# A dense SiLU block on one core: block 1 of x loaded behind the first w1 group, block 0 multiplied alone

## The chip, the core and the metric

The kernel runs on one core of one Trainium2 chip. The metric is the device time of one execution in microseconds (us). Five runs of the kernel before gave 127.13, 127.39, 127.45, 128.46 and 128.78, so the median is 127.45. Beside them there is one profiled execution, from which all durations below are taken.

## The reference

```python
# x: 1 x 2048 x 640, w1: 640 x 1728, w2: 1728 x 640, all bfloat16
def reference(x, w1, w2):
    h = jnp.einsum("bsd,df->bsf", x, w1)
    h = _silu(h)
    out = jnp.einsum("bsf,fd->bsd", h, w2)
    return out
```

## The kernel before

**Names.** S = 2048 rows of x, D = 640 features (DT = 5 tiles of 128), F = 1728 hidden units (FT = 13 full tiles of 128 and a tail of 64). The rows of x are cut into NSC = 4 chunks of 512. `xT` holds x transposed (features on partitions), `w1s` and `w2s` the weights, `hT` the hidden layer, transposed. PSUM has 8 banks, handed out in turn by `bank()`.

**Work.** TensorE (PE) multiplies in two phases. In the first, each tile of 128 hidden units is accumulated over the 5 feature tiles, with w1 as the stationary operand and `xT` streamed; ScalarE (ACT) applies SiLU on the way from PSUM to `hT`. In the second phase the hidden layer is multiplied with w2; VectorE (DVE) and ACT bring results out of PSUM, and SyncE (SP) issues the stores. Chunks 1 to 3 of x arrive transposed by transposing loads (line 149). Chunk 0 is loaded as it is, in blocks of 128 rows (`x0`), and turned on PE against an identity matrix.

**The lead-in**, which the change is about, is an order written out by hand:
- Line 124 loads block 0 of x on SP's queue; line 125 loads block 1 on ACT's queue. Line 126 puts ACT's share of the start-up barrier behind that load. All loads go through the helper at line 89.
- Lines 127 to 131 load w1 in four groups of hidden tiles on SP's queue, `G = [(0, 2), (2, 5), (5, 9), (9, 13)]` (320, 480, 640 and 720 KB). Line 132 loads blocks 2 and 3 of x behind them. After these come the 15 transposing loads of line 149 and the loads of w2.
- Lines 193 and 197 run `dummies(n)`: n matmuls over a tile of zeros, 256 columns each, whose result nobody reads (line 164).
- `turn(j, b_v, b_a)` (lines 166 to 190) waits for block j, transposes its five 128 x 128 tiles into PSUM (line 173), and copies them to `xT`: three tiles on DVE (line 176), two on ACT (line 184), or all five on DVE where both banks are the same.
- `half(ft, m, c0)` (line 216) multiplies m hidden tiles, from tile ft on, with 256 rows of x from row c0 on, and gives the bank to SiLU. All matmuls are recorded under line 200, all of these SiLUs under line 204.
- Line 230 waits for blocks 0 and 1 to be turned; the loop at line 232 then does all 13 tiles on rows 0 to 255, with a wait for the w1 group before each step and the turns of blocks 2 and 3 behind tiles 9 and 11.

[...]

Of the kernel before, what the change touches and what calls it, by code (L numbers as in the profile page):

```python
# [9 lines left out]
def bass_standalone__dense_activation_silu__prompt_kernel(  # L10
# [13 lines left out]
    P = 128  # L24
    NB = 8
    BANK = 512
    DT = D // P
# [3 lines left out]
    HB = 256  # L31
# [6 lines left out]
    pe, act, dve, pool, sp = nc.tensor, nc.scalar, nc.vector, nc.gpsimd, nc.sync  # L38

    with ExitStack() as es:  # L40
        def sb(name, shape, dtype):
            return es.enter_context(nc.sbuf_tensor(name, shape, dtype))

        xT = sb("xT", [P, DT, S], bf16)
        x0 = sb("x0", [P, SCH // P, D], bf16)
        w1s = sb("w1s", [P, DT, F], bf16)
        w2s = sb("w2s", [P, FT, D], bf16)
        w2t = sb("w2t", [P, D], bf16)
        hT = sb("hT", [P, FT, S], bf16)
# [6 lines left out]
        ps = es.enter_context(nc.psum_tensor("ps", [P, NB, BANK], fp32))  # L56
# [4 lines left out]
        def sem(name):  # L61
            s = es.enter_context(nc.semaphore(name))
            count[s.name if hasattr(s, "name") else name] = 0
            return [s, 0]

        def tick(ins, s, n=1):
            ins.then_inc(s[0], n)
            s[1] += n
            return (s, s[1])

        def wait(eng, *points):
            for pt in points:
                if pt is None:
                    continue
                s, v = pt
                key = (id(eng), id(s))
                if seen.get(key, 0) < v:
                    eng.wait_ge(s[0], v)
                    seen[key] = v

        s_pe, s_act, s_dve = sem("s_pe"), sem("s_act"), sem("s_dve")
# [4 lines left out]
        def load(eng, out_ap, in_ap):  # L86
            s = sem(f"s_ld{n_dma[0]}")
            n_dma[0] += 1
            return tick(eng.dma_start(out=out_ap, in_=in_ap), s, 16)  # L89

        ET = mybir.EngineType

        def preamble(engine, opcode):
            lst = nc.main_func.blocks[0].instructions
            return next(
                i for i, ins in enumerate(lst)
                if ins.opcode == opcode and ins.engine == engine
            )
# [12 lines left out]
        def barrier_wait_here(engine):  # L111
            lst = nc.main_func.blocks[0].instructions
            lst.append(lst.pop(preamble(engine, "EventSemaphore")))

        x_v = xf.rearrange("(j p) d -> p j d", p=P)
# [5 lines left out]
        ld_x = {}  # L121
        ld_w1 = {}
        p_z = ahead_of_start(lambda: tick(dve.memset(z[:, :], 0.0), s_dve), ET.DVE)  # L123
        ld_x[0] = load(sp, x0[:, 0, :], x_v[:, 0, :])
        ld_x[1] = load(act, x0[:, 1, :], x_v[:, 1, :])
        barrier_wait_here(ET.Activation)
        for a, b in G:
            e = F if b == FT else b * P
            pt = load(sp, w1s[:, :, a * P:e], w1_v[:, :, a * P:e])
            for ft in range(a, b):  # L130
                ld_w1[ft] = pt
        ld_x[2] = ld_x[3] = load(sp, x0[:, 2:4, :], x_v[:, 2:4, :])
        barrier_wait_here(ET.SP)

        p_warm = tick(pool.memset(warm[:, :], 0.0), s_pool)
        p = tick(pool.memset(ident[:, :], 0.0), s_pool)
# [9 lines left out]
        for c in range(1, NSC):  # L146
            s = sem(f"s_xc{c}")
# [14 lines left out]
        def dummies(n):  # L162
            for _ in range(n):
                pe.matmul(ps[:, 3, 0:HB], lhsT=z[:, 0:P], rhs=z[:, :], start=True, stop=True)  # L164

        def turn(j, b_v, b_a):
            wait(pe, ld_x[j], p_ident, bank_free[b_v], bank_free[b_a])
            v = ps[:, b_v, :].bitcast(bf16)
            a = ps[:, b_a, :].bitcast(bf16)
            nv = DT if b_a == b_v else 3  # L170
            for dt in range(DT):
                dst = v[:, dt * P:(dt + 1) * P] if dt < nv else a[:, (dt - nv) * P:(dt - nv + 1) * P]
                ins = pe.transpose(dst, x0[:, j, dt * P:(dt + 1) * P], ident[:, :])  # L173
            t = tick(ins, s_pe)
            wait(dve, t)
            r = tick(dve.tensor_copy(  # L176
                out=xT[:, 0:nv, j * P:(j + 1) * P],
                in_=v[:, 0:nv * P].rearrange("p (k s) -> p k s", s=P),
            ), s_dve)
            bank_free[b_v] = r  # L180
            pts = [r]
            if nv < DT:
                wait(act, t)
                r = tick(act.copy(  # L184
                    out=xT[:, nv:DT, j * P:(j + 1) * P],
                    in_=a[:, 0:(DT - nv) * P].rearrange("p (k s) -> p k s", s=P),
                ), s_act)
                bank_free[b_a] = r
                pts.append(r)
            return pts  # L190

        wait(pe, p_z)
        dummies(7)
        barrier_wait_here(ET.PE)
        t0 = turn(0, 7, 6)
        t1 = turn(1, 5, 4)
        dummies(2)

        def mm(o, l, r, start, stop, shared=False):
            return pe.matmul(o, lhsT=l, rhs=r, start=start, stop=stop, skip_group_check=shared)  # L200

        def silu(out_ap, in_ap, bank, after):
            wait(act, after)
            r = tick(act.activation(out=out_ap, in_=in_ap, func=ACT.Silu), s_act)  # L204
            bank_free[bank] = r
            return r
# [3 lines left out]
        def bank():  # L210
            b = nxt[0] % NB
            nxt[0] += 1
            wait(pe, bank_free[b])
            return b

        def half(ft, m, c0):
            b = bank()
            for i in range(m):
                for k in range(DT):
                    ins = mm(  # L220
                        ps[:, b, i * HB:(i + 1) * HB],
                        w1s[:, k, (ft + i) * P:(ft + i + 1) * P],
                        xT[:, k, c0:c0 + HB],
                        start=(k == 0 and i == 0), stop=(k == DT - 1), shared=True,
                    )
            t = tick(ins, s_pe)
            silu(hT[:, ft:ft + m, c0:c0 + HB],
                 ps[:, b, 0:m * HB].rearrange("p (m s) -> p m s", m=m), b, t)

        wait(pe, *t0, *t1)  # L230
        tb = []
        for ft, m in [(0, 2), (2, 1), (3, 2), (5, 2), (7, 2), (9, 1), (10, 1), (11, 1), (12, 1)]:
            wait(pe, ld_w1[ft])
            half(ft, m, 0)
            if ft in (9, 11):
                b = bank()
                tb.extend(turn(2 if ft == 9 else 3, b, b))
# [3 lines left out]
        for c in range(1, NSC):  # L241
            wait(pe, ld_xc[c])
            for ft in range(FT):
                b = bank()
                for k in range(DT):
                    ins = mm(ps[:, b, :], w1s[:, k, ft * P:(ft + 1) * P],
                             xT[:, k, c * SCH:(c + 1) * SCH], start=(k == 0), stop=(k == DT - 1))
                h_last = silu(hT[:, ft, c * SCH:(c + 1) * SCH], ps[:, b, :], b, tick(ins, s_pe))
        h_tail = []
        for q in range(NSC // 2):  # L250
            b = bank()
            for k in range(DT):
                for hh in range(2):
                    c = 2 * q + hh
                    ins = mm(ps[hh * FL:(hh + 1) * FL, b, :], w1s[:, k, F0:F],
                             xT[:, k, c * SCH:(c + 1) * SCH],
                             start=(k == 0), stop=(k == DT - 1), shared=True)
# [18 lines left out]
        for c in range(NSC):  # L276
            b = bank()
            wbank.append(b)
            for ft in range(FT):
                mm(ps[:, b, :], w2s[:, ft, DA:D], hT[:, ft, c * SCH:(c + 1) * SCH],  # L280
                   start=(ft == 0), stop=False)
# [59 lines left out]
        for q in range(NSC // 2):  # L341
            tt = []
            for hh in range(2):
                c = 2 * q + hh
# [3 lines left out]
            for hh in range(2):  # L348
                c = 2 * q + hh
# [42 lines left out]
```

## Time and profile before

| What | Value |
|---|---|
| Profiled execution, its own time | 127.13 us |
| Span from its first to its last instruction | 125.7 us |
| Median of five runs (lowest, highest) | 127.45 us (127.13, 128.78) |
| PE matmuls L200, w1 phase (345) | 59.8 us busy |
| PE matmuls L200, w2 phase, `hT` streamed (221) | 45.4 us busy |
| PE dummies L164 (9) | 2.3 us busy, mean 418 ns |
| PE transposes L173 (20) | 2.1 us busy, mean 264 ns |
| HBM read, written | 5.16 MB, 2.62 MB |

Times are counted from the first instruction of the span. PE is tensor matmuls, PEld the loads of their stationary operand, which overlap the matmuls. Matmuls are pipelined: the duration of one is longer than the distance to the next, so the pace is read from the number of instructions in a stretch of time. A DMA row says from which queue a transfer was issued (SPq, ACTq); q1 and q10 are the rings that serve SP's and ACT's queues. A row of the timeline gives start, length, engine, line, operation, tiles and count, and in brackets the idle time before it and what ended it.

### The profile page before, as it was taken

How to read it: one execution, taken by the hardware profiler on the slowest of the kernel's cores; microseconds unless marked ns; L12 is line 12 of the kernel's file. 1: busy time of each engine (PE TensorE's matmuls, PEld its weight loads, DVE VectorE, ACT ScalarE, POOL GpSimd, SP SyncE). 2: the span in 40 equal slices, each digit the busy share in tenths (PEclk: the TensorE clock that was granted, in tenths of full speed). 3: DMA queues.
4: the chain of work that ended last, by engine and by line, in shares of the span. 5: the costliest groups of instructions: out<-in, count | busy, mean ns of one | idle time of the engine just before them, and what ended most of it. 6: DMA issues, size and time to landing. Idle time of an engine off the chain costs nothing.

```text
span 125.7 us, 1522 instructions
## 1 busy us (share of the span) xinstructions
PE 122.5 (97%) x668; PEld 62.3 (50%) x668; DVE 9.2 (7%) x16; ACT 40.3 (32%) x71; POOL 0.8 (1%) x7
## 2 busy tenths in 40 slices
PE   8899999999999999999999999999999999999993
PEld 5589886444444444444444443444344444444452
DVE  0101100000000000000000004202020210012021
ACT  5256456555555555555540003010101011010100
POOL 2000000000000000000000000000000000000000
DMA  6999535479600000000000000542111111111112
GB/s 188 344 383 202 92 87 115 91 160 389 228 1 0 0 0 3 0 5 0 0 0 0 0 0 16 114 124 75 52 52 52 52 52 52 57 52 52 52 55 102
DMA packets 17830, 10.37 MB, mean 83 GB/s; under 512 B 10784, under 2 KB 17824, under 8 KB 17824
## 3 DMA queue, kind: packets, MB, share of 16 engines
q1 hardware_dynamic: 17536, 10.05, 27.5%
q10 hardware_dynamic: 288, 0.23, 0.6%
q8 instruction: 5, 0.08, 0.3%
q14 instruction: 1, 0.01, 0.0%
HBM read 5.16 MB, written 2.62 MB: 62 GB/s over the span
## 4 chain that ended last, share of the span: by engine, by line
PE 95%; DMA 3%; SPq 0%; issue 0%; ACT 0%
PE ps L200 94%; DMA w1s<-in_w_dram 3%; PE ps L173 0%; SPq L89 0%; ACT o_sb L269 0%; SPq L377 0%
## 5 line engine op out<-in xcount | busy, mean ns | idle before, releaser
L200 PE MATMUL ps<-xT,w1s 128*128 128x512 bf16 (+2 forms) x345 | 59.8, 342 | 0.6 <-DMA w1s<-in_w_dram 0.5
L200 PEld LDWEIGHTS ps<-xT,w1s 128*128 128x128 bf16 (+1 forms) x345 | 32.9, 99 | 27.1 <-DVE xT L176 1.3
L200 PE MATMUL ps<-w2s,hT 128*128 128x512 bf16 (+2 forms) x221 | 45.4, 367 | 0.0
L204 ACT ACTIVATE hT<-ps 128x512 bf16<-128x512 f32 (+1 forms) x55 | 31.4, 574 | 27.6 <-PE ps L200 27.6
L200 PEld LDWEIGHTS ps<-w2s,hT 128*128 128x128 bf16 x221 | 20.9, 98 | 24.4 <-issue 1.1
L269 ACT CAST o_sb<-ps 128x512 bf16<-128x512 f32 (+1 forms) x8 | 4.4, 546 | 42.2 <-PE ps L200 42.2
L200 PE MATMUL ps<-hT,w2s 128*128 128x512 bf16 x52 | 11.4, 379 | 0.0
L267 DVE CAST o_sb<-ps 128x512 bf16<-128x512 f32 (+1 forms) x9 | 6.1, 677 | 39.9 <-PE ps L200 39.9
L200 PEld LDWEIGHTS ps<-hT,w2s 128*128 128x128 bf16 x52 | 5.0, 97 | 6.3 <-issue 0.4
L267 DVE CAST oT<-ps 128x512 bf16<-128x512 f32 x2 | 1.3, 686 | 63.4 <-PE ps L200 63.4
L269 ACT CAST oT<-ps 128x512 bf16<-128x512 f32 x2 | 1.1, 588 | 11.1 <-PE ps L200 11.1
L164 PE MATMUL ps<-z 128*128 128x256 bf16 x9 | 2.3, 418 | 0.4 <-DVE z L123 0.4
L176 DVE COPY xT<-ps 128x384 bf16<-128x384 bf16 (+1 forms) x4 | 1.7, 425 | 10.9 <-PE ps L173 10.9
L173 PE MATMUL ps<-ident,x 128*128 128x128 bf16 x20 | 2.1, 264 | 0.2 <-DMA x<-in_x_dram 0.2
L200 PE MATMUL ps<-w2t,hTt 64*128 64x512 bf16 (+2 forms) x17 | 2.2, 366 | 0.0
L173 PEld LDWEIGHTS ps<-ident,x 128*128 128x128 bf16 x20 | 1.6, 116 | 0.8 <-DMA x<-in_x_dram 0.7
L204 ACT ACTIVATE hTt<-ps 128x512 bf16<-128x512 f32 x2 | 1.2, 597 | 1.1 <-PE ps L200 1.1
L143 ACT ACT_TABLE_LOAD x1 | 1.3, 1283 | 0.7 <-PEq L377 0.7
L164 PEld LDWEIGHTS ps<-z 128*128 128x128 bf16 x9 | 1.1, 142 | 0.7 <-DVE z L123 0.4
L200 PEld LDWEIGHTS ps<-w2t,hTt 64*128 64x128 bf16 x17 | 0.7, 94 | 1.4 <-issue 0.8
L184 ACT COPY xT<-ps 128x256 bf16<-128x256 bf16 x2 | 0.7, 372 | 1.0 <-PE ps L173 1.0
L200 PE MATMUL ps<-hTt,w2t 64*128 64x512 bf16 x4 | 0.6, 382 | 0.0
(10 smaller groups left out, 1.5 us busy)
## 6 DMA issues: line engine op xcount, KB each, us to landing
out_dram<-o_sb SPq DMA_DIRECT2D x15, 160.0 KB, 1.8
w2s<-in_w_dram SPq DMA_DIRECT2D x1, 1120.0 KB, 6.0
w2s<-in_w_dram SPq DMA_DIRECT2D x1, 960.0 KB, 8.9
w1s<-in_w_dram SPq DMA_DIRECT2D x1, 720.0 KB, 7.2
w1s<-in_w_dram SPq DMA_DIRECT2D x1, 640.0 KB, 5.9
w1s<-in_w_dram SPq DMA_DIRECT2D x1, 480.0 KB, 4.8
w1s<-in_w_dram SPq DMA_DIRECT2D x1, 320.0 KB, 3.9
x<-in_x_dram SPq DMA_DIRECT2D x1, 320.0 KB, 7.0
```

The costliest lines, as they stand in the source:

```text
L143: act.activation(out=warm[:, :], in_=warm[:, :], func=ACT.Silu)
L164: pe.matmul(ps[:, 3, 0:HB], lhsT=z[:, 0:P], rhs=z[:, :], start=True, stop=True)
L173: ins = pe.transpose(dst, x0[:, j, dt * P:(dt + 1) * P], ident[:, :])
L176: r = tick(dve.tensor_copy(out=xT[:, 0:nv, j * P:(j + 1) * P], in_=v[:, 0:nv * P].rearrange("p (k s) -> p k s", s=P),), s_dve)
L184: r = tick(act.copy(out=xT[:, nv:DT, j * P:(j + 1) * P], in_=a[:, 0:(DT - nv) * P].rearrange("p (k s) -> p k s", s=P),), s_act)
L200: return pe.matmul(o, lhsT=l, rhs=r, start=start, stop=stop, skip_group_check=shared)
L204: r = tick(act.activation(out=out_ap, in_=in_ap, func=ACT.Silu), s_act)
L267: r = tick(dve.tensor_copy(out=out_ap, in_=in_ap), s_dve)
L269: r = tick(act.copy(out=out_ap, in_=in_ap), s_act)
```

## The change

Block 1 of x is loaded on SP's queue, between the first and the second w1 group, no longer on ACT's queue; the line that moved ACT's barrier goes with it. The dummies at the start become 9, and 3 follow the turn of block 0 where 2 followed the turn of block 1. The first two hidden tiles are no longer multiplied with 256 rows at once: `first_block(ft, j)` multiplies hidden tile ft with the 128 rows of block j, and four calls fill the same bank. Between them block 1 is turned. The order on PE is now: 9 dummies, turn of block 0, 3 dummies, tile 0 on block 0, turn of block 1, tile 1 on block 0, a wait for block 1's copies, tile 0 and tile 1 on block 1, then the loop as before from tile 2 on. In the changed file the matmuls carry line 199 and the SiLUs of `half` line 203.

```diff
--- before.py
+++ after.py
@@ -122,13 +122,13 @@
         ld_w1 = {}
         p_z = ahead_of_start(lambda: tick(dve.memset(z[:, :], 0.0), s_dve), ET.DVE)
         ld_x[0] = load(sp, x0[:, 0, :], x_v[:, 0, :])
-        ld_x[1] = load(act, x0[:, 1, :], x_v[:, 1, :])
-        barrier_wait_here(ET.Activation)
         for a, b in G:
             e = F if b == FT else b * P
             pt = load(sp, w1s[:, :, a * P:e], w1_v[:, :, a * P:e])
             for ft in range(a, b):
                 ld_w1[ft] = pt
+            if a == 0:
+                ld_x[1] = load(sp, x0[:, 1, :], x_v[:, 1, :])
         ld_x[2] = ld_x[3] = load(sp, x0[:, 2:4, :], x_v[:, 2:4, :])
         barrier_wait_here(ET.SP)
 
@@ -190,11 +190,10 @@
             return pts
 
         wait(pe, p_z)
-        dummies(7)
+        dummies(9)
         barrier_wait_here(ET.PE)
         t0 = turn(0, 7, 6)
-        t1 = turn(1, 5, 4)
-        dummies(2)
+        dummies(3)
 
         def mm(o, l, r, start, stop, shared=False):
             return pe.matmul(o, lhsT=l, rhs=r, start=start, stop=stop, skip_group_check=shared)
@@ -227,9 +226,25 @@
             silu(hT[:, ft:ft + m, c0:c0 + HB],
                  ps[:, b, 0:m * HB].rearrange("p (m s) -> p m s", m=m), b, t)
 
-        wait(pe, *t0, *t1)
+        def first_block(ft, j):
+            for k in range(DT):
+                c = ft * HB + j * P
+                ins = mm(ps[:, 0, c:c + P], w1s[:, k, ft * P:(ft + 1) * P],
+                         xT[:, k, j * P:(j + 1) * P],
+                         start=(k == 0 and ft == 0 and j == 0), stop=(k == DT - 1), shared=True)
+            return ins
+
+        bank()
+        wait(pe, *t0, ld_w1[0])
+        first_block(0, 0)
+        t1 = turn(1, 5, 4)
+        first_block(1, 0)
+        wait(pe, *t1)
+        first_block(0, 1)
+        t = tick(first_block(1, 1), s_pe)
+        silu(hT[:, 0:2, 0:HB], ps[:, 0, :].rearrange("p (m s) -> p m s", m=2), 0, t)
         tb = []
-        for ft, m in [(0, 2), (2, 1), (3, 2), (5, 2), (7, 2), (9, 1), (10, 1), (11, 1), (12, 1)]:
+        for ft, m in [(2, 1), (3, 2), (5, 2), (7, 2), (9, 1), (10, 1), (11, 1), (12, 1)]:
             wait(pe, ld_w1[ft])
             half(ft, m, 0)
             if ft in (9, 11):
```

## The prediction

> **What bounds the kernel now.** I read the page's engine totals first, then the chain of waits in order of time, then the timeline of the first 16 us, then the transfers there. The totals name the engine:
>
> ```profile
> PE 122.5 (97%) x668; PEld 62.3 (50%) x668; DVE 9.2 (7%) x16; ACT 40.3 (32%) x71; POOL 0.8 (1%) x7
> ```
>
> TensorE (PE) is busy for 122.5 of 125.7 us, so only the lead-in can hold a loss. The chain (start us, length us, what) shows it:
>
> ```profile
> 0.09 0.39 SPq L89
> 0.47 0.06 issue
> 0.53 3.85 DMA w1s<-in_w_dram
> 4.38 0.14 issue
> 4.52 6.24 PE ps L200 x50
> 10.76 0.28 PE ps L173 x5
> 11.04 1.09 PE ps L200 x10
> 12.13 0.28 PE ps L173 x5
> ```
>
> The first w1 group is issued at 0.53, lands at 4.38, and the first real matmul starts at 4.52. Ten matmuls over 256 columns then take 1.09, so one goes every 0.109 us; five 128-column transposes take 0.28, or 0.056 each. Fifty at 0.109, of which the last lasts 0.27, would be 5.61; the row says 6.24. The missing 0.63 lies at the start, as two windows show (length, then PE busy, then weight loads):
>
> ```profile
> 4.51:5.74 1.23, 1.22 (x6) 0.87 (x7) 0.00 (x0) 0.00 (x0) 0.00 (x0) 1.00 1.08 366
> 6.23:7.76 1.53, 1.53 (x17) 1.36 (x14) 0.00 (x0) 0.93 (x2) 0.00 (x0) 1.00 1.08 387
> ```
>
> Fourteen loads fit in 1.53 (0.109 each), but only six matmuls in 1.23, about 0.21 each. Some 6 matmuls cost 0.104 too much: 0.63. The clock column says 1.00 in both windows, so the two paces are read from the instructions alone. The pace doubles near 5.8. Before that:
>
> ```profile
> 0.39 1.68 PE L164 MATMUL ps<-z 128*128 128x256 bf16 x7 [0.39 <-DVE z L123]
> 2.29 1.26 PE L173 MATMUL ps<-ident,x 128*128 128x128 bf16 x10 [0.22 <-DMA x<-in_x_dram]
> 3.04 0.36 DVE L176 COPY xT<-ps 128x384 bf16<-128x384 bf16 x1 [2.70 <-PE ps L173]
> 3.04 0.37 ACT L184 COPY xT<-ps 128x256 bf16<-128x256 bf16 x1 [0.79 <-PE ps L173]
> 3.34 0.63 PE L164 MATMUL ps<-z 128*128 128x256 bf16 x2
> 4.52 6.24 PE L200 MATMUL ps<-xT,w1s 128*128 128x256 bf16 x50 [0.54 <-DMA w1s<-in_w_dram]
> ```
>
> Seven dummies in 1.68, the last lasting 0.42, go every 0.21; ten transposes about every 0.107, half the pace they have at 10.76. PE stands still for 0.22 before block 0 and 0.54 before w1. The transfers set that last gap and the deadlines behind it (KB, us from issue to landing):
>
> ```profile
> w1s<-in_w_dram SPq DMA_DIRECT2D x1, 640.0 KB, 5.9
> w1s<-in_w_dram SPq DMA_DIRECT2D x1, 480.0 KB, 4.8
> x<-in_x_dram SPq DMA_DIRECT2D x1, 320.0 KB, 7.0
> ```
>
> With issues at 0.99, 1.56 and 3.19, w1 group 2 lands at 5.8, group 3 at 7.5 and x blocks 2 and 3 at 10.2. In the window 1.1 to 2.5 the ACT queue (q10, x block 1) shares the 16 DMA engines with SP's (q1):
>
> ```profile
> q1 hardware_dynamic: 295, 0.24, 61.3%
> q10 hardware_dynamic: 144, 0.16, 33.6%
> ```
>
> **The change, part by part.** All of it is made against this execution: 127.13 us with a span of 125.7, the fastest of five, 0.32 under their median. My yardstick is when the group of row tile 2 can start: 10.76 less one duration (0.27) less 39 x 0.109 = 6.24.
>
> *Block 1 leaves the ACT queue and goes behind w1 group 1.* q10's packets took 33.6% of 1.4 us = 0.47 us of all engines, mostly ahead of w1's. So group 1 lands up to 0.47 sooner, and not sooner at all if issue-to-first-packet time holds it. I take 0.40, nearer the busy end because the two shares together, 94.9% over the window, leave little idle: landing 3.98, first matmul 0.14 later (as now) at 4.12. Block 1 then lands when all the bytes before it have: still 4.38, usable at 4.52; bounds 4.3 and 4.85 (a full 0.47 behind an unmoved group 1).
>
> *The later issues on SP.* Block 1's issue (0.39 on ACT) is inserted there, so w1 groups 2 to 4, x blocks 2 and 3, all 15 transposing loads and the w2 loads are issued 0.4 later. Their bytes wait behind the same bytes as before, so I cost the landing at 0, with 0.4 as the other end. Margins: group 2 is wanted at 6.24, landing 5.8; group 3 at 6.24 + 15 x 0.109 = 7.88, landing 7.5; the transposing loads have microseconds; w2 is first read at 64.6 and issued near 25. The cover is thin only for group 3: 0.4 less 0.14, some 0.25 us, and no gain larger than that survives it. On ACT nothing waits: its table load runs from 0.73 to 2.01 and its first copy starts at 3.04.
>
> *Dummies 7 to 9 and 2 to 3.* Nine from 0.39 issue until 0.39 + 9 x 0.213 = 2.31; block 0's transposes started at 2.29, so this costs 0.02 and fills the 0.22 gap. Transposes until 2.85, three dummies until 3.49; both copies of block 0 end near 3.43. All lie before 4.12 and cost nothing; were w1 there at 3.5 the last dummy would begin to show.
>
> *Ten matmuls of 256 columns become twenty of 128, with block 1's transposes on the path.* At the pace of that moment, 0.107 per 128 columns until about 5.8 and 0.056 after:
> - Row tile 0 on block 0: 4.12 + 5 x 0.107 = 4.65. Block 1 is usable at 4.52, so no wait.
> - Transposes: 4.65 + 0.53 = 5.19; the last ends 0.2 later (it lasts 0.31). Copies: 5.39 + 0.02 + 0.37 = 5.78. From a copy's end to a matmul the later turn shows 0.10: 5.88.
> - Row tile 1 on block 0 issues from 5.19 to 5.72, beneath the copies; PE then idles 0.16. The new wait holds only the ten matmuls behind it and the first silu.
> - Ten matmuls: 5.88 + 10 x 0.056 = 6.44.
>
> That is 0.20 after 6.24. Earlier w1 gives 0.40; the transposes, formerly under the w1 wait, cost 0.53; the idle 0.16 is added, and the matmuls themselves take 0.10 less (1.62 for 1.72) because ten of them fall behind 5.8: -0.40 + 0.53 + 0.16 - 0.10 = 0.19. So 127.13 + 0.20 = 127.33.
>
> The moment when the pace doubles is not shown for the changed order, so I bound it. If at 3.8: 4.40, wait to 4.52, transposes to 4.80, copies to 5.35, matmuls from 5.45 to 6.01, that is -0.23, just inside group 3's limit. If only after the block: ten at 0.107 end at 6.95, +0.71, and 0.104 more for each later matmul at the slow pace. PE idles less here before 4.1 than now and about 0.2 more after, so I keep 5.8 for the sum and both ends for the range.
>
> [...]
>
> **Rivals.**
> 1. *The first w1 group does not land sooner* (first packets are late, not crowded out). For: block 0's row shows transfers with a long fixed part, 2.2 us for 160 KB. Against: the 94.9% above. Then 4.38 and block 1 at 4.85: 4.52, 5.05, 5.59, copies to 6.18, matmuls 6.28 to 6.84: +0.60, 127.7; with the five runs' 0.32, 128.0.
> 2. *Slower: the pace doubles late*, because transposes and the wait for the copies now break up the stretch from 4.1 to 5.9 that now is plain matmul. Price: 0.51 on the block, 0.104 per matmul after it. To be 1% above the median (128.72) it needs 1.39 over 127.33: the block and 9 matmuls more, a doubling after 6.95 + 9 x 0.213 = 8.9. For it: the five times spread over 1.65 us, which something varying must make. Against: PE does as much work before 5.9 as now. Time 128.8.
> 3. *Faster by more than the lead-in's slack.* It takes under 126.18. Group 3's landing forbids more than 0.25 (126.88), and the same early doubling would give the kernel before 0.25 too. It needs loads landing 0.7 sooner, which nothing here does.
>
> **How the numbers follow.** My forecast, doubling somewhere between 3.8 and 6.4 with transfers as above, covers 126.9 to 127.65 and gets 0.66; I name 127.3. Rival 1 gets 0.17 (127.7 to 128.0), rival 2 0.12, rival 3 0.05. The range goes from the floor that group 3 sets, 126.85, to 128.6, just under rival 2, and so leaves out rivals 2 and 3. About 1% (1.27 us) is what a measurement can tell from no change: forecast and rival 1 stay within it, 0.83; slower 0.12, faster 0.05.
>
> **What would show it.** In the profile after: a w1 landing near 4.0 and a first L199 matmul near 4.1 (rival 1: 4.5); five transposes near 4.65; a PE gap of about 0.16 ended by a copy of xT; the first silu near 6.6, and everything behind it 0.2 later than now. A silu before 6.3 says that the pace doubled early; 128-column matmuls still 0.107 apart after 6.5 say rival 2. A PE wait for w1 at row tile 5, near 7.6, would mean that group 3 sets the time. I am wrong outright if anything behind 13 us changes length.

## The result, and the profile after

The changed kernel takes 128.45 us (median of 43 runs, 127.67 to 130.40), the kernel before 128.04 (80 runs, 126.97 to 130.48). The ratio is 1.0046, 95% interval 1.0029 to 1.0063: slower by half a per cent, or 0.59 us of 128.04. The means of all runs, 128.57 and 128.04, give 1.0042. The five times of before that the prediction started from were low ones: their median is 127.45, of all 80 runs only 39 lie under 128.0, and the profiled 127.13 is near the bottom. The ratios leave out runs more than 1.5% above the fastest of their kernel, among them executions in which PE's pace doubled late (one of 131.22 us, described below, at 12.6), so figures of all runs stand beside the ratio where it matters.

The profiled execution of the changed kernel took 129.46 us with a span of 128.0, so it is at the slow end of its own spread; two more profiles of it stand below. Its chain of waits in order of time (start, length, what):

```profile
0.53 3.80 DMA w1s<-in_w_dram
4.33 0.14 issue
4.47 0.69 PE ps L199 x5
5.16 0.53 PE ps L173 x5
5.69 0.53 PE ps L199 x5
6.22 0.02 issue
6.24 6.83 PE ps L199 x50
13.08 0.28 PE ps L173 x5
```

w1 group 1 lands at 4.33, hardly earlier than before (4.38). Behind it stand the three fives of the new order (tile 0 on block 0, the transposes of block 1, tile 1 on block 0), all at the slow pace: 0.53 for five, 0.107 each (the first row, 0.69, has the length of its last matmul in it). Then the timeline around row tile 2 (start, length, engine, operation, count, idle time before and what ended it):

```profile
6.21 0.99 PEld L199 LDWEIGHTS ps<-xT,w1s 128*128 128x128 bf16 x10 [0.26 <-DVE xT L176]
7.42 5.38 PEld L199 LDWEIGHTS ps<-xT,w1s 128*128 128x128 bf16 x40 [0.22 <-DMA w1s<-in_w_dram]
7.50 0.60 ACT L203 ACTIVATE hT<-ps 128x512 bf16<-128x512 f32 x1 [1.41 <-PE ps L199]
```

The wait for block 1's copies is there, and a second wait that the first profile of before did not have: PE waits for w1 group 2 before tile 2. The loads say why (KB, us from issue to landing):

```profile
w1s<-in_w_dram SPq DMA_DIRECT2D x1, 640.0 KB, 7.0
w1s<-in_w_dram SPq DMA_DIRECT2D x1, 480.0 KB, 5.8
...
x<-in_x_dram SPq DMA_DIRECT2D x1, 320.0 KB, 8.3
```

Group 2 is issued at 1.56 and lands at 7.37, where before it was issued at 0.99 and landed at 5.77. By its own pace PE would have been ready for tile 2 at 7.26; it starts at 7.42. The windows give the state of the DMA engines (the share is the last but one number) and the pace on PE:

```profile
3.50:4.50 1.00, 0.21 (x2) 0.07 (x2) 0.00 (x0) 0.00 (x0) 0.00 (x0) 1.00 0.69 169
4.50:5.50 1.00, 1.00 (x11) 1.00 (x12) 0.00 (x0) 0.00 (x0) 0.00 (x0) 1.00 0.97 260
7.42:9.74 2.32, 2.32 (x12) 1.64 (x12) 0.00 (x0) 0.98 (x2) 0.00 (x0) 1.00 1.08 387
9.74:11.93 2.19, 2.19 (x21) 1.97 (x20) 0.00 (x0) 1.05 (x2) 0.00 (x0) 1.00 1.43 221
```

From 3.5 to 4.5 the engines are busy for 0.69 of the time. And the pace doubles only at 9.7: twelve weight loads in 2.32 us, then twenty in 2.19. Ten matmuls of 256 columns behind tile 2 run at 0.213.

### The profile page after: what moved, and what is told of

Same layout as the page of the kernel before. It is cut to its first block, busy times and chain, and to the rows that moved or that the text cites. A ratio compares the mean times of both kernels' runs of the same rounds, so it can differ in the third digit from the quotient of the medians.

```text
span 128.0 us, 1548 instructions
## 1 busy us (share of the span) xinstructions
PE 124.7 (97%) x681; PEld 64.1 (50%) x681; DVE 9.2 (7%) x16; ACT 40.4 (32%) x71; POOL 0.8 (1%) x7
## 4 chain that ended last, share of the span: by engine, by line
PE 95%; DMA 3%; SPq 0%; issue 0%; ACT 0%
PE ps L199 94%; DMA w1s<-in_w_dram 3%; PE ps L173 1%; SPq L89 0%; ACT o_sb L284 0%; SPq L392 0%
## 5 line engine op out<-in xcount | busy, mean ns | idle before, releaser
L199 PE MATMUL ps<-xT,w1s 128*128 128x512 bf16 (+3 forms) x355 | 61.9, 344 | 0.9 <-DMA w1s<-in_w_dram 0.8
L199 PEld LDWEIGHTS ps<-xT,w1s 128*128 128x128 bf16 (+1 forms) x355 | 34.2, 102 | 27.9 <-DVE xT L176 1.8
L199 PE MATMUL ps<-hT,w2s 128*128 128x512 bf16 x52 | 11.4, 379 | 0.0
L164 PE MATMUL ps<-z 128*128 128x256 bf16 x12 | 2.9, 419 | 0.4 <-DVE z L123 0.4
L164 PEld LDWEIGHTS ps<-z 128*128 128x128 bf16 x12 | 1.6, 144 | 0.9 <-DVE z L123 0.4
```

## The experiments

**The parts of the change, one at a time.** Order alone:

```diff
-        ld_x[1] = load(act, x0[:, 1, :], x_v[:, 1, :])
-        barrier_wait_here(ET.Activation)
...
+            if a == 0:
+                ld_x[1] = load(sp, x0[:, 1, :], x_v[:, 1, :])
```

> The kernel before with the load order alone changed: block 1 of x on SP's queue between w1 groups 1 and 2; dummies 7 and 2, both turns and 256-column matmuls as before. Queue theory (block 1 on SP's queue keeps the DMA engines short of packets, so w1 group 2 lands near 7.4 us as in the profile after, against 5.8 before): ratio above 1.004, here more than in the changed kernel, since both turns stand in front of the first matmul, 129 us or more. Compute-order theory (the transposes on the path and the 128-column matmuls cost the time, the landings are accidents of one execution): the wait for block 1 still delays the first matmul from 4.5 to about 5.7, so some 1.0 to 1.2 us, but w1 group 2 lands near 6. The landing of group 2 in the profile tells them apart.

Measured: ratio 1.0089 (1.0060 to 1.0118), median 129.46. Group 2 landed at 7.09, block 1 at 4.81. Both theories had a loss here; the landing is near the 7.4 of the queue theory and not near 6. This order alone is worse than the whole change: with both turns in front, the first matmul waits for block 1. PE stands still for 1.69 us until it has landed, and the two dummies behind that turn start only at 5.37, as the timeline shows:

```profile
4.86 0.71 PE L173 MATMUL ps<-ident,x 128*128 128x128 bf16 x5 [1.69 <-DMA x<-in_x_dram]
5.37 0.63 PE L164 MATMUL ps<-z 128*128 128x256 bf16 x2
6.27 2.08 PE L200 MATMUL ps<-xT,w1s 128*128 128x256 bf16 x9 [0.27 <-ACT xT L184]
```

The whole change without its load order (block 1 back on ACT's queue, at line 125 of before):

> The changed kernel with block 1 loaded on ACT's queue again, so that all that is left of the change is 9 and 3 dummies and block 0 multiplied alone, with block 1 turned in between. Queue theory: groups 2 and 3 land near 5.8 and 7.5 again, the loss is gone, ratio 0.995 to 1.001. Compute-order theory: the loss stays, ratio 1.003 to 1.007.

Measured: 0.9982 (0.9953 to 1.0011), median 128.08. The time is what the queue theory said, but the landing is not: group 2 landed at 7.67 in this profile, with the loads of before. And the changed kernel, run beside it, had 1.0008 (0.9973 to 1.0043, below), so these intervals do not separate the kernel with the moved load from the one without it.

Dummies alone:

```diff
-        dummies(7)
+        dummies(9)
...
-        dummies(2)
+        dummies(3)
```

> The kernel before with 9 and 3 dummies in place of 7 and 2, nothing else. Queue theory and compute-order theory: no loss, ratio 0.997 to 1.001. Pace theory (how long PE stays at the slow pace of 0.21 us for a 256-column matmul decides most of the spread between executions, and more dummies make it double earlier): the upper half of the times, near 128.5, gets rarer, ratio 0.994 to 0.998.

Measured: 0.9934 (0.9910 to 0.9959), seven runs, 127.39 to 128.03. Three dummies make the kernel faster by 0.7%, and no run lies in the upper half of the times of before, near 128.5. The timeline of its profile:

```profile
4.44 1.59 PE L200 MATMUL ps<-xT,w1s 128*128 128x256 bf16 x10
6.07 0.60 ACT L204 ACTIVATE hT<-ps 128x512 bf16<-128x512 f32 x1 [1.88 <-PE ps L200]
6.89 2.11 PEld L200 LDWEIGHTS ps<-xT,w1s 128*128 128x128 bf16 x20 [1.14 <-DMA w1s<-in_w_dram]
6.90 2.27 PE L200 MATMUL ps<-xT,w1s 128*128 128x256 bf16 x19 [0.86 <-DMA w1s<-in_w_dram]
```

The first ten matmuls take 1.59; in the first profile of before they took 1.88 (4.52 to 6.40). The pace has doubled early, near 5.2. Then PE waits 0.86 us for group 2, and the landing is the bound.

The split alone (block 0 multiplied alone, block 1 turned in between; dummies 7 and 2, block 1 on ACT's queue):

> The kernel before with the split alone: block 0 multiplied alone and block 1 turned in between; block 1 on ACT's queue, dummies 7 and 2. Compute-order theory: the transposes after w1's landing cost 0.4 to 0.7 us of PE's chain, and the stretch that doubles the pace is broken up, so that more executions lie above 128.2: ratio 1.002 to 1.006. Landing theory: PE waits for group 2 anyway, ratio 0.998 to 1.002.

Measured: 1.0101 (1.0038 to 1.0164), six runs, 128.28 to 129.88; the means of all runs give 1.0090. This is more than either theory gave. Its chain of waits:

```profile
4.30 0.69 PE ps L199 x5
4.99 0.53 PE ps L173 x5
5.52 0.53 PE ps L199 x5
6.05 0.02 issue
6.08 6.27 PE ps L199 x50
```

All three fives are slow, and the last ten too: 6.08 to 6.99 for their starts. The pace doubled at 8.4 in this execution.

The changed kernel again, twice:

> The changed kernel again, for a second profile. Queue theory: w1 group 2 lands after 7.0 and group 3 after 8.7 again, whatever the moment at which the pace doubles. If these landings were an accident of the first profile, they are near 5.8 and 7.5 here. Ratio 1.003 to 1.007 either way.

> The changed kernel a third time, beside the others. Ratio 1.001 to 1.007, w1 group 2 landing at 6.8 to 7.4, DMA engines' share under 0.85 from 3.5 to 4.5 us.

Measured: 1.0008 (0.9973 to 1.0043) and 1.0037 (1.0003 to 1.0071), medians 128.27 and 128.25. In both the pace doubled early, near 5.5 and 4.9, and group 2 landed at 6.88 and 7.22. The first of the two misses what was expected of it, by a little: the landing is under 7.0 and the ratio under 1.003. In the second the timeline reads:

```profile
5.86 0.72 PE L199 MATMUL ps<-xT,w1s 128*128 128x128 bf16 x10 [0.28 <-ACT xT L184]
6.61 0.60 ACT L203 ACTIVATE hT<-ps 128x512 bf16<-128x512 f32 x1 [0.90 <-PE ps L199]
7.26 1.53 PEld L199 LDWEIGHTS ps<-xT,w1s 128*128 128x128 bf16 x15 [0.86 <-DMA w1s<-in_w_dram]
7.26 1.98 PE L199 MATMUL ps<-xT,w1s 128*128 128x256 bf16 x16 [0.69 <-DMA w1s<-in_w_dram]
```

Here the new order finishes its 20 matmuls early (0.72 for the last ten) and has nothing from it: PE stands still for 0.69 until group 2 is there.

**Is group 2 late because of the change?** The kernel before again:

> The kernel before again, for a second profile. Landing theory (w1 group 2 lands near 7 us in most executions of every version so far, and the 5.8 of the first profile of before was the fortunate end; the span is then the start of row tile 2 plus 119.5 us plus 0.104 for each later slow matmul): group 2 lands at 6.8 to 7.7 here, PE waits for it for 0.3 to 1.2 us behind its first ten matmuls, and the span is above 126.3. Queue theory (only the moved load of block 1 makes group 2 late): group 2 lands near 5.8 again. Ratio 0.998 to 1.002.

> A third profile of the kernel before. If its loads land group 2 earlier than the changed order does: at 5.7 to 6.8. If one spread holds for all versions: as likely above 6.8 as below.

> A second profile of the dummies-only kernel (9 and 3), the same loads as the kernel before. If the loads decide: group 2 at 5.7 to 6.9. If PE's work at the start bears on the landing: 6.8 to 7.7 again, as in the three profiles with more dummies or the split.

Measured: the second profile of before has group 2 at 6.70 (ratio 0.9975, 0.9940 to 1.0011, which must be 1), the third at 5.74 with a span of 125.3, and the dummies-only kernel at 6.93. Neither "always near 7" nor "always early" holds for the kernel before. The 6.93 lies just outside what was expected if the loads decide, and inside what was expected if PE's work at the start bears on the landing. What goes with the landing of group 2 is how early the execution's first load, block 0, lands:

| Profile | block 0 lands | group 2 lands | tile 2 starts | span | span less start |
|---|---|---|---|---|---|
| before, first | 2.24 | 5.77 | 6.23 | 125.66 | 119.4 |
| before, third | 2.28 | 5.74 | 5.84 | 125.31 | 119.5 |
| before's loads, 9 and 3 dummies | 2.48 | 6.85 | 6.90 | 126.39 | 119.5 |
| the same, second | 2.61 | 6.93 | 6.98 | 126.49 | 119.5 |
| before, second | 2.65 | 6.70 | 6.75 | 126.26 | 119.5 |
| before's loads, split alone | 2.81 | 7.21 | 7.26 | 127.23 | 120.0 |
| changed, first | 2.26 | 7.37 | 7.42 | 127.99 | 120.6 |
| changed, second | 2.41 | 6.88 | 6.93 | 126.46 | 119.5 |
| changed, third | 2.26 | 7.22 | 7.26 | 126.78 | 119.5 |

The span is the start of tile 2 plus 119.5, and 0.104 more for each later matmul at the slow pace (some ten in the first changed profile: 1.04). With before's loads, group 2 lands at 5.75 where block 0 lands before 2.3, and at 6.3 to 7.7 where it lands after 2.45 (three profiles that are not in the table among them). With the changed loads it lands at 7.2 to 7.4 although block 0 lands at 2.26. So it seems that the change takes away the fortunate executions, in which group 2 is about 1.5 us later. This rests on two profiles of before against three with the changed loads (one of them a kernel described below), and it is not isolated: the two early ones have 7 and 2 dummies, the three late ones 9 and 3. Every profile with before's loads and 9 and 3 dummies or more has group 2 at 6.85 or later, those with 7 and 2 have 5.74 to 7.21. Against the dummies as the sole cause stands one profile, the load order alone with 7 and 2 dummies: block 0 at 2.41, group 2 at 7.09. In the other executions the profiles are too few to see a difference. The same second, from 3.5 to 4.5, in the third profile of before:

```profile
3.50:4.50 1.00, 0.76 (x5) 0.25 (x4) 0.36 (x1) 0.37 (x1) 0.00 (x0) 1.00 1.06 354
```

The engines are full at 1.06 and move 354 GB/s, against 0.69 and 169 GB/s above. But with before's loads they can be idle too, as in the kernel with block 1 on ACT's queue:

```profile
3.50:4.50 1.00, 0.94 (x7) 0.45 (x5) 0.36 (x1) 0.37 (x1) 0.00 (x0) 1.00 0.76 205
```

The three profiles of the changed kernel have 0.69, 0.75 and 0.76 there, the two of the dummies alone 0.82 and 0.81. In these six, and in the two early ones of before, shares of 0.69 to 0.82 go with a group 2 at 6.85 to 7.67, and 1.03 and 1.06 with 5.77 and 5.74; with 11 and 6 dummies, below, 0.96 goes with 7.11. So idle engines in this second do not point to the moved load.

**What makes it late?** Four kernels were made to say it, and none settled it. The first has w1 group 2 on ACT's queue; it also has 9 and 3 dummies, and ACT's share of the barrier stands behind the loads:

```diff
+            pt = load(act if a == 2 else sp, w1s[:, :, a * P:e], w1_v[:, :, a * P:e])
```

> The kernel before with 9 and 3 dummies, and w1 group 2 issued on ACT's queue behind block 1 of x. Against the same dummies with all of w1 on SP's queue (ratio 0.993). If one queue cannot hand out packets fast enough to keep the DMA engines busy from 3.5 to 5 us, group 2 now lands before 6.3 and the ratio falls to 0.985 to 0.991. If the late landing comes from the DMA engines themselves, group 2 still lands near 7 and the ratio stays at 0.991 to 0.996.

Measured: 1.0009 (0.9961 to 1.0057), runs from 127.09 to 131.22, outside both expectations. In the profile, which is of its slowest execution, group 2 landed at 8.07, later than anywhere, with the DMA engines at 0.9 or more in every half microsecond from 3.5 to 5.5 (291 to 364 GB/s). Group 3 landed at 8.38 on SP's queue, 0.31 behind it, where with both on SP's queue it landed 1.7 behind (7.5 after 5.77 in the first profile of before). So in this profile group 2 seems to have shared the engines with group 3.

An extra load of 160 KB that nobody reads, on SP between groups 1 and 2, or on ACT behind block 1 (dummies 9 and 3 in both):

```diff
+            if a == 0:
+                load(sp, xd[:, :], x_v[:, 1, :])
```

> The dummies-only kernel (9 and 3) with one load more, 160 KB that nobody reads, on SP's queue between w1 groups 1 and 2, where the changed kernel has block 1; PE's order is as in the kernel before. Queue theory: DMA engines idle from 3.5 to 4.5 us (busy share 0.6 to 0.8) and group 2 lands near 7.4 or later; ratio 0.997 to 1.002, 0.3% or more above the same load on ACT's queue. If only the bytes count: same ratio as on ACT's queue, about 0.997, which is 0.993 plus 0.47 us of packets.

> The dummies-only kernel (9 and 3) with the same extra 160 KB on ACT's queue behind block 1, so the same bytes stand in front of w1 group 2. Queue theory: the DMA engines stay at a share of 0.9 or more from 3.5 to 4.5 us, group 2 lands near 7.0, ratio 0.994 to 0.998. If only the bytes count: about 0.997, equal to the kernel with the load on SP's queue.

Measured: 0.9979 (0.9950 to 1.0008) on SP with group 2 at 6.51, and 0.9963 (0.9934 to 0.9991) on ACT with group 2 at 6.80. The two do not differ, and on SP the engines' share from 3.5 to 4.5 was 0.97. So one more issue in front of group 2 did not make it later here (6.51 for 6.85 and 6.93 with the dummies alone); the queue theory as I had put it falls.

The changed kernel with 160 KB that nobody reads on ACT's queue, where block 1 was:

> The changed kernel with one load more: 160 KB that nobody reads, on ACT's queue at the start, where block 1 was before. Idle theory (without an early load on ACT's queue the DMA engines have nothing to do in parts of 1.5 to 4.5 us, since SP's packets come too late): the engines' share stays at 0.9 or more there, group 2 lands at 6.5 to 6.9 in spite of the 160 KB more, ratio 0.998 to 1.003. Bytes theory (the engines are the bound): group 2 lands 0.4 later than in the changed kernel, at 7.3 to 7.8, ratio 1.006 to 1.010.

Measured: 1.0057 (1.0011 to 1.0102). In the profile, again of its slowest execution (130.47), group 2 landed at 7.06 with the share at 0.96: between both expectations. Group 2 is no later for the extra bytes, so the engines seem to have had idle time, but group 1 landed at 4.99, the pace doubled only near 11.4, and the time is no better than the changed kernel's.

**What is PE's order worth without the loads?** Both kernels were run with tiles 2 to 12 of rows 0 to 255 taken from the columns of tiles 0 and 1, and with blocks 0 and 1 read in the turns of blocks 2 and 3, so that the same work is done without a wait for the later loads (the result is another, only the time counts):

```diff
+        def wcol(ft, c0):
+            return (ft % 2 if c0 == 0 else ft) * P
...
-            wait(pe, ld_w1[ft])
+            wait(pe, ld_w1[0])
```

> The changed kernel with the later loads taken out of the lead-in: on rows 0 to 255 the hidden tiles 2 to 12 are multiplied with the columns of tiles 0 and 1 (w1 group 1), and the turns of blocks 2 and 3 read blocks 0 and 1 again, so PE waits for nothing behind block 1 until row 256. All loads are still made. What remains is the PE chain and its pace. Landing theory: this falls clearly under the changed kernel (ratio to before 0.990 to 0.996), and lies within 0.3% of the kernel before changed in the same way. Compute-order theory: it is slower than that one by 0.4% or more.

> The kernel before with the same taken out: tiles 2 to 12 on rows 0 to 255 with the columns of tiles 0 and 1, the turns of blocks 2 and 3 from blocks 0 and 1. Landing theory: ratio 0.988 to 0.996, since the wait for group 2 is gone. Queue theory (group 2 was never late in the kernel before): ratio 0.998 to 1.001. What is left of the spread between executions then belongs to the moment at which the pace doubles.

Measured: 0.9927 (0.9891 to 0.9964) for the changed order, median 127.28; 0.9939 (0.9884 to 0.9994) for the order before, median 128.22. The runs fall into two groups, and these say more than the medians:

| | early group | late group |
|---|---|---|
| order before | 126.42 to 126.76 (4 of 12, one more at 127.54) | 128.16 to 128.88 (7) |
| order changed | 126.81 to 127.34 (8 of 12) | 128.87 to 129.16 (4) |

Without waits for the later loads it seems to be the pace that makes two groups: in the profile of the early group it doubled at 3.7, in that of the late group of the changed order at 8.9. Group against group the changed order costs 0.5 to 0.6 us (means 127.11 for 126.52, and 128.99 for 128.51), and it has fewer late runs; over all runs the two do not differ (means 127.74 and 127.77). Taking the later loads out of the lead-in is worth 0.8 us to the changed kernel by the means of all runs (128.57 to 127.74; 1.2 by the medians, 128.45 to 127.28), though these are two sets of runs, and 0.4 to the kernel before (128.15 beside it to 127.77).

**More dummies, and finer groups.** 11 and 6 dummies, then these with w1 in five groups, then the five groups with 9 and 3:

```diff
-        G = [(0, 2), (2, 5), (5, 9), (9, FT)]
+        G = [(0, 2), (2, 4), (4, 7), (7, 10), (10, FT)]
...
-            if ft in (9, 11):
+            if ft in (10, 11):
```

> The kernel before with 11 dummies at the start and 6 behind the turn of block 1 (7 and 2 before; 9 and 3 in the dummies-only kernel, whose ratio was 0.993). PE then works without a gap from 0.4 us to the first real matmul, which starts near 5.1 where w1 lands at 4.3. Pace theory: the doubling comes before 6 in every execution, the upper group of times (above 128.2) is gone, ratio 0.991 to 0.995; the 0.6 us by which the first matmul starts later costs nothing, as row tile 2 waits for w1 group 2 until 6.7 or later. If the dummies are only work in the way: ratio above 0.997 and the first silu later than tile 2 can start.

> The kernel with 11 and 6 dummies, and w1 in five groups (hidden tiles 0-1, 2-3, 4-6, 7-9, 10-12) in place of four, with the turns of blocks 2 and 3 one step later (behind tiles 10 and 11) because these blocks land near 11.3, just as PE arrives. Landing theory: the second group is 320 KB in place of 480 and lands some 0.4 us sooner, the first matmul on tile 2 with it; ratio 0.2 to 0.4% under the kernel with 11 and 6 dummies alone. If the landing of the second group does not set the time, the two are equal.

> The kernel before with 9 and 3 dummies, w1 in five groups and the turns of blocks 2 and 3 one step later. With 11 and 6 dummies the first matmul started at 5.07 and nothing waited for a group; here it starts near 4.45, so tile 2 near 5.8. Landing theory: third group (landing 6.7) and fourth (8.05) become the next waits, the gain is 0.2 to 0.4%, ratio 0.990 to 0.994. If the pace doubles late in more executions with fewer dummies: 0.994 to 0.998.

Measured: 0.9965 (0.9936 to 0.9994), 0.9951 (0.9922 to 0.9981) and 0.9952 (0.9915 to 0.9989). The first and the last gained less than the better of their expectations, and the finer groups are 0.14% under the same dummies without them, which these intervals do not separate. With 11 and 6 the upper group did not vanish (four of 12 runs at 128.25 to 128.40); the pace doubled at 4.6 in its profile and group 2 landed at 7.11, so landing alone puts a run at 128.15. With five groups PE works through, as one row of the timeline shows:

```profile
5.07 6.54 PE L200 MATMUL ps<-xT,w1s 128*128 128x256 bf16 x55
```

No wait for a group is left among these 55, and no run of this kernel (11 and 6 dummies, five groups) is above 127.93. The median with five groups and 9 and 3 dummies is 127.10 where the kernel before had 127.90 beside it: this version beats both kernels. That its fewer dummies are better or worse than 11 and 6 is not shown, the intervals being the same.

## Why the prediction was wrong

The time lies in the range that was given, 126.85 to 128.6, and within the 1% that had 0.83. But the forecast of 127.3 against 127.45 was no change, and the change is a clear loss of 0.46%. By its steps:

1. *The yardstick.* One execution was taken for the kernel. Its group 2 landed at 5.8 and its pace doubled near 5.8. The third profile of before is like it (5.74, and a doubling at 5.3), but the second has 6.70 and a doubling at 7.0. The median of 80 runs is 0.9 above that execution, where I had 0.32.
2. *"Landing 3.98"* for w1 group 1. Failed: 4.33, 3.73 and 4.21, on average 4.09 against 4.14 in the three profiles of before (4.38, 4.00, 4.05). The gain of 0.40 was 0.05 on average. The first half of rival 1 is what happened, and block 1 landed 0.4 behind, at 4.78, 4.11 and 4.59.
3. *"I cost the landing at 0, with 0.4 as the other end"* for the later loads on SP. This is the step that failed. I argued that their bytes wait behind the same bytes, so group 2 had to land at 5.8, or 6.2 at the other end, ahead of the 6.44 at which my sum had tile 2 start. It landed at 7.37, 6.88 and 7.22, and tile 2 started just behind it each time, at 7.42, 6.93 and 7.26, where PE by its own pace would have been ready at 7.26, 6.20 and 6.41. The margin that I had listed, 6.24 against 5.8, was 0.44, and it came from a fortunate execution: 6.70 in the second profile of before would have used it up without any change. I took the thin cover to be group 3; it was group 2 (PE waits 0.05 for group 3 in the second and third profiles). How much of the lateness is the moved load's and how much the spread that before has too is not shown. In favour of the load are the 1.5 us between executions whose block 0 lands equally early (7.2 to 7.4 for 5.75) and the 1.0089 of the load order alone, which also has a wait for block 1 in it. In time, 0.9982 without the moved load and 1.0008 with it, beside each other, are not apart; 1.0037 and 1.0046 come from other sets of runs.
4. *The order on PE, +0.20 against the profile.* The mechanism was right: from group 1's landing to the readiness of tile 2 I had 2.46, and the profiles show 2.93, 2.48 and 2.21 by their pace, for 1.86 before. The wait for the copies was there with 0.22 to 0.44 us between the pace's next slot and the next start, for my 0.16. The gain of an earlier w1 fell away, and without it the sum is the +0.60 of rival 1; group against group, in the kernels without waits for loads, the order costs 0.5 to 0.6.
5. *"I keep 5.8"* for the doubling of the pace. Mis-sized in spread, not in sign: 9.7, 5.5 and 4.9 in the three profiles. Rival 2, a late doubling, is what the first profile of the changed kernel shows, by 8.9 or later as I had asked for. The dummies that I costed at nothing are worth 0.66% by themselves, and the split alone costs 1.0%; together, without the moved load, they leave 0.9982, no change that can be told.
6. *"PE idles less here before 4.1 than now and about 0.2 more after"*. On this I kept 5.8, and rival 2 made the transposes and the wait the cause of a late doubling. That idle time, or breaks in the plain matmuls, sets the moment was my estimate, and no run isolates it. The runs show the pace going from 0.213 to 0.109 at moments between 3.7 and 12.6 us. It is late where PE waited (12.6 in the kernel with group 2 on ACT, where PE stood still from 7.3 to 8.1), but it varies without that: the two kernels with 11 and 6 dummies, which do the same work up to 5 us, have 4.6 and 5.8. Between the early and the late group of the kernels without waits for loads lie 2.0 us in the order before and 1.9 in the changed one. The split alone has its transposes between its first matmuls and all six runs above 128.2, but it also waits for its copies. The runs have a gain with the dummies and a loss with the split; that these come by the moment of the doubling is not shown.

So the half per cent looks like a balance: -0.66% from the dummies and about +1.0% from the split, which together leave -0.18% (interval through 0), and +0.3 to +0.6% from block 1's move (0.3% within one set of runs on one chip, where it is within the noise). That these add up is not shown: they share one wait, and PE's order costs nothing where group 2 lands behind its end, as in the third profile of the changed kernel, where PE stands still for 0.69. Open is why group 2 is late by 1.5 us where its issue is only 0.57 later, and whether the moved load alone does it. The four kernels above speak against the simple answers, that it is the issue as such, the bytes, or the missing load on ACT's queue. The pair that would settle it, the changed kernel with and without the moved load, has one profile without it, and in that one block 0 landed late (2.77) and group 2 at 7.67.

## What to carry to other kernels

Profile a kernel with a load-bound lead-in more than once before costing a change to it: look up when its first load landed and when its pace doubled, and sort the executions by these before taking one as the yardstick. Of a moved load, count the margin of every later load on the same queue against the latest landing seen, not against the one in the profile at hand. Work without use that fills PE's waits before the first real matmul can be worth more than another order of the real work: here three dummies gave 0.7%.

## What the runs showed of the hardware

- The profile's granted clock says 1.00 in stretches where matmuls of 256 columns go every 0.213 us and in those where they go every 0.109 (in the first changed profile from 7.42 to 9.74 and from 9.74 to 11.93).
- Once doubled, the pace survived waits of PE of 0.7 to 1.3 us in four profiles (0.69 in the third of the changed kernel, 0.86 with the dummies alone, 1.04 with 11 and 6 dummies, from 6.4 to 7.7 in the changed kernel with block 1 on ACT's queue).
- The same 480 KB behind the same loads, issued at 0.99, landed after 4.7 to 6.7 us in nine profiles. It went with the landing of a load of 160 KB at the very start: 5.75 where that landed at 2.24 and 2.28, and 6.3 to 7.7 where it landed at 2.46 to 2.81.
- Issued on a second queue at 0.62, group 2 landed at 8.07 in the one profile of it, where it landed at 6.85 and 6.93 on the first queue with the same dummies; the DMA engines were at 0.9 or more, with 291 to 364 GB/s from 3.5 to 5.5, against 0.82 and 0.81 from 3.5 to 4.5.
